# A multi-query attention kernel whose instruction order is written down as tables, with five short stretches ordered anew

## The chip, the cores and the metric

One NeuronCore of one Trainium2 chip runs the whole program. The metric is the device time of one execution in microseconds. The kernel before has a median of 664.33 us over three runs (664.21 to 664.44).

A core has engines that each take their own instruction list in order: TensorE (PE, matrix products into eight PSUM banks), ScalarE (ACT), VectorE (DVE), GpSimd (POOL) and SyncE (SP, which here only starts transfers). They meet through semaphores. Transfers are carried out by 16 DMA engines.

## The reference

```python
def reference(A_x, A_wq, A_wk, A_wv, A_wo, B_x, B_w1, B_b1, B_w2, B_b2):
    def _A_ref(x, wq, wk, wv, wo):               # S=2048, D=640, H=32, Dh=20
        q = (x @ wq).reshape(B, S, H, Dh).transpose(0, 2, 1, 3)
        k = x @ wk                               # one key head for all 32 heads
        v = x @ wv
        scores = jnp.einsum("bhqd,bkd->bhqk", q, k) * (Dh ** -0.5)
        p = _softmax(scores, axis=-1)
        o = jnp.einsum("bhqk,bkd->bhqd", p, v)
        return o.transpose(0, 2, 1, 3).reshape(B, S, H * Dh) @ wo
    def _B_ref(x, w1, b1, w2, b2):               # F=1536
        h = jnp.einsum("bsd,df->bsf", x, w1) + b1
        r = jnp.where(h > 0, h, 0)
        return jnp.einsum("bsf,fd->bsd", r * r, w2) + b2
    xn = _layernorm(A_x)
    return A_x + _A_ref(xn, A_wq, A_wk, A_wv, A_wo) + _B_ref(xn, B_w1, B_b1, B_w2, B_b2)
```

Attention and a feed-forward layer work on the same normalised input, and both are added to it. Softmax over 32 x 2048 x 2048 scores is the bulk.

## The kernel before

**Tiles and units.** The queries are cut into four chunks of 512, the heads into eight groups of four. That makes 32 blocks, each with 16 key tiles of 128 keys. A block and a key tile make a *unit*, numbered 16 x block + key tile (0 to 511). A unit has four score tiles, one per head, of 128 keys x 512 queries, numbered 4 x unit + head. A score tile fills one PSUM bank.

**Two ways to the exponential.** Most tiles go to ScalarE: a pair of score matmuls fills two banks, and one instruction (line 1328) takes the exponential of both into two slots of the buffer `PT`. Four matmuls, one per head, then multiply a unit of `PT` with the values (`PT,vx` in the profile) into the accumulator of the block. The other 164 units, here called *sets*, go to VectorE: it evicts each of the four banks (line 1551) with a multiply, an add and a conversion to 16-bit integers, whose bits read as bf16 are a piecewise linear exponential. To smooth it, three *passes* add one, two and three quarters of an octave to those bits in further buffers: on POOL (`int64_add`, line 1571), two passes joined in one instruction (line 2121), or on VectorE (line 1572). Thus a set has four *terms*, 0 to 3, and the sum of the four, with weights 1, 1, 0.707 and 0.707 held in `vx` and `vxs`, is the exponential.

**Pair sums.** Each term costs TensorE a group of four matmuls. To save groups, term 0 may be added into term 1, and term 3 into term 2, before they are multiplied. This is done by an accumulating DMA that POOL issues (line 1588 for 0 into 1, line 2047 for 3 into 2, 512 KB each; line 2119 for both in one transfer of 1024 KB), or by an addition on VectorE.

**Names.** In what follows an instruction is named as the change's tables name it:
- `q:` a pair of score tiles for ScalarE, `d:unit.head` a score tile for VectorE, `a:` an exponential on ScalarE, `e:unit.head` an eviction on VectorE;
- `p:unit.j` a pass, `j:unit.2` the joined passes 2 and 3;
- `s:unit.0` and `s:unit.3` the sums of 0 into 1 and of 3 into 2, `b:unit.3` both in one transfer;
- `v:unit` the multiplication of a ScalarE unit with the values, `u:unit.term` that of one term. The reader of `s:108.0` is `u:108.1`, that of `s:366.3` is `u:366.2`;
- `fill` and `warm`: matmuls with zeros whose result does not matter. `FFN`, `FP`, `OUT`, `QC` and the like are the parts of the projections and of the feed-forward layer, which stand between the attention work.

All matmuls go through the helper in line 729, so all have that line in the profile.

**What sets the order.** While the program is built, a planner goes step by step through a modelled time: class `Op` (line 251) holds each instruction with its engine, duration and dependences, and tables of rules and priorities decide which instruction comes next on which engine. Its result is then rearranged by `PLAN`, one text of indices for each engine, which `unpack` (line 290, called at line 2086) turns into an order; further texts choose which variant of a sum or pass is used, and on which VectorE instruction a POOL instruction has to wait because the two share a port (`held`). Then `replay` (line 300, called at line 2146) goes through the order with modelled durations and landings of transfers, and gives out PSUM banks, `PT` slots and term buffers. From the dependences the program derives the waits.

Landings there are a model, with constants near the head of the file:

```python
ADLATE = 0.6
ADLEAD = 1.24
ADLAND = 4.36
ADGAP = 2.73
```

Of the kernel before, what the change touches and what calls it, by code (L numbers as in the profile page):

```python
# [17 lines left out]
HPG = 4  # L18
# [20 lines left out]
def _pl(z):  # L39
# [9 lines left out]
NB = 7  # L49
PVB = 7  # L50
SHARED = (4, 5, 6)
SIDES = ((0, 1), (2, 3))
POOLED = tuple(range(NB))
HELD = sum(SIDES, ())
EVP = 0.8
JIT = 0.7
MRG = 9
M1 = 9
M1T = 0
ADDN = 0.5  # L60
R3 = 2
NOPEN = 2
SETW = HPG * 512
NL = 5
NT = 10
DRATE = 0.95
DLAST = 3.5
DSLACK = 0
URG = 4
PBIAS = 5  # L70
DGAP = 1.5
DMARG = 3.8
DMEND = 2.5
SLX = 5.0
CMX = 2.0
XRLAT = 6.2
NADS = 8
ADDUR = 0.905
ADPL = 0.3
ADM = 0.7  # L80
ADMP = 0.7
ADLATE = 0.6
ADLEAD = 1.24
SPF, SPG, SPT = 1.3, 0.84, 560.0
DWQ, DWO, DWB, DWS, DWM, DWOD, DOFF = 0.02, 0.22, 0.16, 0.02, 0.16, 1.0, 1.28
ADLAND = 4.36
ADGAP = 2.73
SWITCH = 0.0985
ACB, ACM = 0.0631, 0.4267
Q1POS = 3  # L90
WARM = 0.72

# [2165 lines left out]
```

## Time and profile before

| | |
|---|---|
| median of three runs | 664.33 us |
| profiled execution, first to last instruction | 663.4 us |
| TensorE busy | 655.2 us (99%) |
| ScalarE busy | 649.3 us (98%) |
| VectorE busy | 627.1 us (95%) |
| POOL busy | 533.1 us (80%) |
| single pair sums (512 KB), median from issue to landing | 5.7 us |
| double pair sums (1024 KB), median from issue to landing | 9.0 us |

The time of the runs lies 0.93 us above the span of the profiled execution; the rest lies before the first and behind the last instruction. In the rows, a line starts with a time or a source line, then the engine, the operation and the program's names `output<-input`; `xN` counts instructions, and what stands in brackets or behind the last bar is idle time of the engine just before them with what ended it. In rows of the timeline the first number is the start and the second the length of all the instructions of the row together.

### The profile page before, as it was taken

The numbers are of one execution on the slowest core, as the hardware profiler recorded it, in microseconds if no ns is written. First come the engines' busy times: TensorE is split into PE (matmuls) and PEld (weight loads), VectorE is DVE, ScalarE is ACT, GpSimd is POOL, SyncE is SP. The second block draws the span as 40 slices with busy tenths as digits, with TensorE's granted clock in tenths as the row PEclk, the third lists the DMA queues.
The fourth block names the chain that finished last, engine by engine and source line by source line (L and its number), as shares of the span: only waits on it lengthen the run. The fifth ranks groups of instructions, "written<-read, shape, count | busy, mean of one in ns | idle before, by whom it ended". The sixth has DMA issues, their size and how long they took to land. (4 is left out here: it accounts for less than half of the span.)

```text
span 663.4 us, 22377 instructions
## 1 busy us (share of the span) xinstructions
PE 655.2 (99%) x9569; PEld 211.9 (32%) x9570; DVE 627.1 (95%) x1125; ACT 649.3 (98%) x719; POOL 533.1 (80%) x528
## 2 busy tenths in 40 slices
PE   8999999999999999999999999999999999999997
PEld 4432222332322223323332222333333322223444
DVE  8979999999999999999999999999999999999997
ACT  7999999999999999999999999999999999999995
POOL 1629899898998889898999988889899999799300
PEclk9999999999999999999999999999999999999999
DMA  8594957788997995696957645798788655858741
GB/s 289 160 241 109 197 119 161 163 183 189 190 191 162 185 179 117 127 182 125 181 105 154 126 91 102 154 180 176 151 170 167 131 126 97 172 104 182 136 111 70
DMA packets 53528, 102.09 MB, mean 154 GB/s; under 512 B 15916, under 2 KB 31164, under 8 KB 53364
## 3 DMA queue, kind: packets, MB, share of 16 engines
q0 software_dynamic: 18544, 68.17, 55.5%
q1 hardware_dynamic: 34164, 31.94, 16.6%
q8 instruction: 75, 1.23, 0.8%
q10 hardware_dynamic: 720, 0.54, 0.3%
q14 instruction: 25, 0.20, 0.1%
HBM read 23.26 MB, written 10.01 MB: 50 GB/s over the span
## 5 line engine op out<-in xcount | busy, mean ns | idle before, releaser
L1328 ACT ACTIVATE PT<-ps 128x1024 bf16<-128x1024 f32 x696 | 640.3, 1121 | 2.2 <-PE ps L729 1.7
L1551 DVE TENSOR_SCALAR tx<-ps 128x512 uint16<-128x512 f32 x656 | 424.0, 683 | 21.1 <-PE ps L729 14.2
L1571 POOL INT64_ADD tx<-tx x369 | 391.2, 1130 | 57.3 <-PE ps L729 16.8
L729 PE MATMUL ps<-qT,kT 20*128 20x512 bf16 x2048 | 262.9, 384 | 0.3
L729 PEld LDWEIGHTS ps<-qT,kT 20*128 20x128 bf16 x2048 | 67.3, 91 | 253.3 <-ACT PT L1328 132.9
L729 PE MATMUL ps<-PT,vx 128*32 128x512 bf16 x1392 | 131.3, 384 | 0.0
L729 PE MATMUL ps<-tx,vxs 128*32 128x512 bf16 x1220 | 112.9, 384 | 0.4 <-DMA tx<-tx 0.3
L1588 POOL DMA_DIRECT2D tx<-tx x103 | 102.8, 998 | 7.7 <-POOL tx L1571 6.9
L729 PE MATMUL ps<-w_sb,big 128*32 128x320 bf16 x1536 | 82.6, 302 | 0.0
L729 PE MATMUL ps<-tx,vx 128*32 128x512 bf16 x864 | 81.0, 384 | 1.6 <-DMA tx<-tx 1.6
L729 PE MATMUL ps<-xnT,w_sb 128*32 128x512 bf16 x960 | 78.9, 383 | 0.0
L1572 DVE TENSOR_SCALAR tx<-tx 128x2048 uint16<-128x2048 uint16 x91 | 63.3, 707 | 0.8 <-DMA tx<-tx 0.5
L729 PEld LDWEIGHTS ps<-PT,vx 128*32 128x32 bf16 x1392 | 34.3, 94 | 39.7 <-issue 35.2
L729 PEld LDWEIGHTS ps<-w_sb,big 128*32 128x32 bf16 x1536 | 34.0, 95 | 31.1 <-issue 20.3
L729 PEld LDWEIGHTS ps<-tx,vxs 128*32 128x32 bf16 x1220 | 28.5, 94 | 36.5 <-issue 27.6
L1054 DVE TENSOR_SCALAR hT_tmp<-ps,b1col 128x512 bf16<-128x512 f32 x48 | 35.7, 743 | 1.6 <-PE ps L729 1.3
L729 PE MATMUL ps<-xnT,wq_sb 128*32 128x512 bf16 (+2 forms) x480 | 35.6, 356 | 0.0
L729 PE MATMUL ps<-wo_c,OC 128*32 128x320 bf16 x576 | 31.8, 301 | 0.0
L2121 POOL INT64_ADD tx<-tx x16 | 30.6, 1913 | 0.5
L729 PEld LDWEIGHTS ps<-tx,vx 128*32 128x32 bf16 x864 | 20.9, 95 | 27.9 <-issue 20.5
L729 PEld LDWEIGHTS ps<-xnT,w_sb 128*32 128x32 bf16 x960 | 19.3, 94 | 25.7 <-issue 17.4
L1416 DVE COPY OR<-ps 128x512 f32<-128x512 f32 x30 | 20.5, 682 | 0.9 <-PE ps L729 0.6
(91 smaller groups left out, 242.6 us busy)
## 6 DMA issues: line engine op xcount, KB each, us to landing
tx<-tx POOLq DMA_DIRECT2D x111, 512.0 KB, 5.7
tx<-tx POOLq DMA_DIRECT2D x7, 1024.0 KB, 9.0
w_sb<-in_B_w_dram SPq DMA_DIRECT2D x8, 480.0 KB, 9.4
big<-OR SPq DMA_DIRECT2D x71, 40.0 KB
xb<-in_A_x_dram SPq DMA_DIRECT2D x1, 2560.0 KB, 12.2
xb<-b2r POOLq DMA_DIRECT2D x1, 2560.0 KB, 19.0
xr<-xb SPq DMA_DIRECT2D x16, 160.0 KB, 3.4
out_dram<-out_sb SPq DMA_DIRECT2D x15, 160.0 KB, 2.9
```

The source lines that it names most:

```text
L729: return lambda e: e.matmul(out_(), l, val(r), start=val(start), stop=val(stop), tile_position=tp, skip_group_check=loose)
L1054: o = Op(f"RL{qc}_{f}", "DVE", 0.66, [lambda e: e.tensor_scalar(out=hT_tmp[:, k % 2, :], in0=ps[:, at(bk), :], scalar1=b1col[:, f:f + 1], ...
L1328: o = Op(f"ACT{st_['j']}", "ACT", ACB + ACM * n, [lambda e: e.activation(out=PT[:, slots[0].n:slots[0].n + n, :], in_=src(), func=AF.Exp, ...
L1416: tn = op(f"TN{b}", "DVE", 0.60, lambda e: e.tensor_copy(out=OR[:, a, :], in_=ps[:, PVB, :]), [lastpv] + or_users[a], prio=0)
L1551: d1 = op(f"D1_{n}_{i}", "DVE", 0.60, lambda e: e.tensor_scalar(out=L()[:, cs].bitcast(U16), in0=ps[:, ref.n, :], scalar1=XA, scalar2=XB, ...
L1571: fns = dict(POOL=lambda e, T=T, j=j: e.int64_add(out=T().bitcast(I64), in0=L().bitcast(I64), in1=TSTEP * j * 0x0001000100010001), DVE=lam ...
L1572: DVE=lambda e, T=T, j=j: e.tensor_scalar(out=T().bitcast(U16), in0=L().bitcast(U16), scalar1=TSTEP * j, scalar2=None, op0=ALU.add))
L1588: p = op(f"AD{a}_{n}", "POOL", ADDUR, lambda e, src=src, dst=dst: e.dma_start(dst(), src(), accum_op=ALU.add), dp + [ad_last.get(k)], dma= ...
L2121: fn = lambda e, x=x: e.int64_add(out=two(*sorted((x["ref"][2].n, x["ref"][3].n))).bitcast(I64), in0=two(*sorted((x["ref"][0].n, x["ref"][ ...
```

## The change

The planner, its rules and `PLAN` are removed, and so is `replay`. In their place stand tables of words: `ORDER` has, for each engine, every instruction by name in its order, with the PSUM banks, `PT` slots or term buffers behind an `@`; `TENANTS` lists for each of the 15 term buffers which terms live in it one after the other; `HELD` has, for each POOL instruction that shares the port, the VectorE instruction that it waits for. Dependences are rebuilt from these. To leave out waits that other waits already cover, the program still needs one order over all engines; it takes it from rough durations.

Nearly everywhere the words stand in the order of before. In five stretches, about 143-172, 227-250, 277-298, 449-470 and 470-491 us of the profile before, TensorE, VectorE, POOL and SP have another order, found by a search in which landings of the sums as recorded took the place of the modelled ones. In detail:
- POOL, in the first four stretches (before, then after):

```
p:108.1 p:110.3 s:108.0 p:109.2 p:107.1 p:108.2 p:106.1 p:109.3 s:107.0 p:106.2 p:107.2 s:106.0 p:106.3 p:127.1 p:126.1 s:127.0
p:108.1 j:108.2 s:108.0 p:110.3 p:109.2 p:109.3 p:106.2 p:107.1 p:106.1 s:107.0 s:106.0 p:106.3 s:127.0 p:107.3 p:126.1 p:126.3 s:126.0

j:172.2 b:172.3 p:171.1
j:172.2 s:172.0 s:172.3 p:171.1

p:222.1 b:222.3 p:223.3 p:221.3 p:220.1
p:222.1 p:223.3 s:222.3 p:221.3 p:221.1 s:222.0 p:221.2 p:220.1 j:220.2 p:219.1 s:220.0

p:367.1 p:367.3 s:367.0 p:365.3 s:366.0 p:365.2 p:366.3 p:364.2 s:365.0 p:364.3 s:366.3 p:364.1
p:367.1 p:366.3 s:367.0 p:367.2 p:366.1 s:366.0 j:365.2 p:364.1 p:366.2 s:365.0 s:366.3 j:364.2
```

- The number of double sums falls from seven to five, that of single sums by DMA rises from 111 to 116. A sum `s:382.3` is new.
- TensorE: score tiles, products and projections are interleaved anew in the stretches, with some other banks; `u:382.3` falls away. Three fills, at 39.33, 40.65 and 597.18 us, are left out.
- VectorE: nine times two evictions become one instruction over two banks, 128 x 1024 (`e:107.32`, `127.01`, `126.23`, `125.32`, `124.10`, `219.01`, `239.31`, `399.02`, `398.30`). Some passes move between VectorE and POOL.
- ScalarE: near 483 us, three pairs in a row (`a:1490`, `a:1492`, `a:1494`) are divided anew over the same six tiles, as three, two and one (`a:1491`, `a:1493`, `a:1495`).

The diff, cut to its core:

```diff
-RC = dict(SAME=0.0027, CR=0.105, RC=0.0995, FIRST=0.011, LANE=0.004, ACT=0.9035, ACTN=0.0165, ...
-def replay(seq, pool, order_all, upool):
...
+ORDER = {
...
+        "p:172.1@14 s:173.0 j:172.2@9,12 s:172.0 s:172.3 p:171.1@11 p:171.2@5 p:171.3@13 p:173.2@4 p:173.3@5 s:171.0 p:191.1@8 s:190.0 p:190.2@0 s:191.0 p:191.2@4 p:189.1@12 p:189.3@5 "
...
+        "p:366.3@0 s:367.0 p:367.2@7 p:366.1@14 s:366.0 j:365.2@6,2 p:364.1@12 p:366.2@7 s:365.0 s:366.3 j:364.2@6,10 p:363.1@2 j:363.2@12,5 p:383.3@1 p:383.1@6 s:363.0 s:383.0 p:382.1@7 "
...
+TENANTS = (
...
+HELD = (
...
-            if e in PLAN:
...
-                seq[e] = [old[k] for k in unpack(PLAN[e], len(old))]
...
+        for _, a, e, ns in planned("e"):
+            u, hs = int(a.split(".")[0]), [int(h) for h in a.split(".")[1]]
+            x = sets.setdefault(u, Terms())
+            i, n = len(x.order), len(hs)
+            refs = [head[HPG * u + h][0] for h in hs]
...
+        for k, a, e, _ in planned("s", "b"):
+            u, j = map(int, a.split("."))
+            x = sets[u]
+            pairs = ((0, 1), (3, 2)) if k == "b" else ((0, 1),) if j == 0 else ((3, 2),)
+            deps = [d for p in pairs for t in p for d in x.made[t]] + (x.reads[1] if j == 0 else [])
...
+        seq = {e: [made[w] for w in names[e]] for e in ENG}
...
+        filler = {(u, j): o for e in ("DVE", "POOL") for o in seq[e] for u, j in o.fills}
+        for n, tenants in enumerate(TENANTS):
+            free_after = list(xn_op.values()) if n >= NMORE else []
+            for k in map(int, tenants.split()):
+                u, j = divmod(k, NTERM)
+                assert sets[u].at[j] == n
+                filler.pop((u, j)).deps += free_after
+                free_after = sets[u].reads[j]
...
+        ROUGH = dict(PE=0.22, ACT=0.95, DVE=0.6, POOL=1.0, SP=0.6)
...
+            free[o.eng] = t + ROUGH[o.eng]
+            when[o] = free[o.eng] + (0.2 if o.dma is None else 4.0)
+            order_all.append(o)
```

More of the change, by code (lines that the diff above doesn't have):

```diff
@@ L48 @@
 PTR = 16
-NB = 7
-PVB = 7
+NSET = 15
+SETW = HPG * 512
 SHARED = (4, 5, 6)
[L52 to L76, printed above, removed]
-NADS = 8
[L78 to L84, printed above, removed]
@@ new lines, in bass_parallel_sum__grouped_kv_mqa__dense_activation_squared_relu__prompt_kernel, with col4, evac_T @@
+        lib_op = op("LIB", "POOL", lambda e: e.load_library(library_config.all_libraries[1]), list(xn_op.values()))
+        def col4(lhs, rhs, n, k, last, bank, m=32, loose=False):
+            return [mm(lambda j=j: ps[32 * j:32 * j + m, at(bank), 0:n], lhs(j), rhs, k == 0, last, (0, 32 * j), loose) for j in range(4)]
+        def evac_T(st, bk, eng, t):
+            cs = slice(128 * st, 128 * st + 128)
+            src = lambda: psbf(bk)[:, 0:DT * 128].rearrange("p (dt n) -> p dt n", dt=DT)
+            if eng == "DVE":
+                te_op[st] = op(f"TE{st}", "DVE", lambda e: e.tensor_copy(out=xnT[:, :, cs], in_=src()), [t])
+            else:
+                te_op[st] = op(f"TE{st}", "ACT", lambda e: e.activation(out=xnT[:, :, cs], in_=src(), func=AF.Identity), [t])
+            return te_op[st]
@@ new lines, in scaled_v, with unit @@
+        def scaled_v(c):
+            cs = slice(4 * c, 4 * c + 4)
+            vs_of[c] = op(f"VS{c}", "DVE", lambda e: e.tensor_scalar(out=vxs[:, cs, :], in0=vx[:, cs, :], scalar1=TW[2], scalar2=None, op0=ALU.mult), [v_of[c]], lock=True)
+        scaled_v(0)
+        def unit(name, chunks, deps, ref):
+            for k, fn in enumerate(chunks):
+                o = op(f"{name}.{k}", "PE", fn, deps if k == 0 else [])
+                if k == 0:
+                    o.takes = [ref]
+            return o
@@ L1926, in bass_parallel_sum__grouped_kv_mqa__dense_activation_squared_relu__prompt_kernel @@
-        assert not misc and unit[0] is None and act_next[0] == len(steps), (len(misc), misc[:1] and misc[0].name, act_next[0], len(steps), pv_blk, cur)
-        assert pv_blk[0] == NBLK and not dve_q and not pool_q and not sp_q, (dve_q, pool_q, sp_q)
-        assert len(fin_ev) == 8
-        MODEL.update(end=max(free.values()), lastact=act_ops[-1].fin, sets=len(sets), steps=len(steps), busy={k: sum(o.dur for o in seq[k]) for k in ENG}, seq=seq, order=order_all)
-        if STOP:
-            raise StopIteration
@@ new lines, in bass_parallel_sum__grouped_kv_mqa__dense_activation_squared_relu__prompt_kernel @@
+        for o in made.values():
+            o.deps = [x for d in o.deps for x in (same[id(d.dma), d.tgt[1]] if d.dma is not None else [d])]
+        giver = {}
+        for o in made.values():
+            for r in o.gives:
+                giver[r] = o
+        bank_rel = dict(first_rel)
+        for o in seq["PE"]:
+            assert len(o.takes) == len(o.banks)
+            for r, n in zip(o.takes, o.banks):
+                r.n = n
+                if n in bank_rel:
+                    o.deps.append(bank_rel[n])
+                bank_rel[n] = giver[r]
```

1943 lines of the change are left out of this document (402 added, 1541 removed), and 445 rows, old and new, of tables (HELD, ORDER, PLAN, TENANTS).

## The prediction

> **What bounds the kernel now.** I read the page first: the busy time of each engine, the granted clock, the groups, the sums.
>
> ```profile
> span 663.4 us, 22377 instructions
> PE 655.2 (99%) x9569; PEld 211.9 (32%) x9570; DVE 627.1 (95%) x1125; ACT 649.3 (98%) x719; POOL 533.1 (80%) x528
> PEclk9999999999999999999999999999999999999999
> ...
> L1328 ACT ACTIVATE PT<-ps 128x1024 bf16<-128x1024 f32 x696 | 640.3, 1121 | 2.2 <-PE ps L729 1.7
> L1551 DVE TENSOR_SCALAR tx<-ps 128x512 uint16<-128x512 f32 x656 | 424.0, 683 | 21.1 <-PE ps L729 14.2
> ...
> tx<-tx POOLq DMA_DIRECT2D x111, 512.0 KB, 5.7
> tx<-tx POOLq DMA_DIRECT2D x7, 1024.0 KB, 9.0
> ```
>
> TensorE and ScalarE are both full: between 20 and 650 us they are busy 627.41 and 628.01 of 630 us.
>
> ```profile
> core 0: us, PE busy (x) PEld busy (x) DVE busy (x) ACT busy (x) POOL busy (x), PEclk, DMA share, GB/s
> ...
> 20.00:650.00 630.00, 627.41 (x9014) 196.14 (x9003) 599.79 (x1038) 628.01 (x684) 529.38 (x518) 1.00 0.74 151
> ```
>
> TensorE writes scores, ScalarE takes the exponential of most of them and hands the bank back, TensorE multiplies the result: neither can run away from the other. What either loses in the middle is therefore lost at the end. Next the list of waits: which transfers did TensorE wait for?
>
> ```profile
> PE ps L729 <- DMA tx<-tx: 1.9, 4, 0.6
> ...
> PEld ps L729 <- DMA tx<-tx: 3.5, 5, 1.0
> ```
>
> Four times, 1.9 us in all, it waited for a pair sum (an accumulating transfer from `tx` to `tx`); its weight load also waited a fifth time. The timeline of TensorE finds them; the readers are `u:106.1`, `u:172.1`, `u:222.2` and `u:366.1`. The fifth, `u:108.1` at 156.2 us, cost TensorE almost nothing.
>
> ```profile
> 164.29 0.40 PE L729 MATMUL ps<-tx,vx 128*32 128x512 bf16 x4 [0.64 <-DMA tx<-tx]
> ...
> 239.71 0.40 PE L729 MATMUL ps<-tx,vx 128*32 128x512 bf16 x4 [0.31 <-DMA tx<-tx]
> ...
> 292.17 0.40 PE L729 MATMUL ps<-tx,vxs 128*32 128x512 bf16 x4 [0.31 <-DMA tx<-tx]
> ...
> 463.80 0.40 PE L729 MATMUL ps<-tx,vx 128*32 128x512 bf16 x4 [0.62 <-DMA tx<-tx]
> ```
>
> The chain of waits goes through the last of these: 8.34 us from issue to landing, and from there on TensorE alone.
>
> ```profile
> 455.42 8.34 DMA tx<-tx
> 463.76 0.04 issue
> 463.80 49.98 PE ps L729 x737
> ```
>
> **The change part by part.** *The bookkeeping* (planner, rules and index tables out, word tables in) runs while the program is built and issues no instruction: 0. Outside five stretches, about 143-172, 227-250, 277-298, 449-470 and 470-491 us of the profile, the four engines and SP's queue have their words in the same order as before, so what follows concerns these, and three fills.
>
> *The five waits.* What do they cost both engines? ScalarE's rows around the two long ones:
>
> ```profile
> 162.49 1.96 ACT L1328 ACTIVATE PT<-ps 128x1024 bf16<-128x1024 f32 x2
> 165.09 1.94 ACT L1328 ACTIVATE PT<-ps 128x1024 bf16<-128x1024 f32 x2 [0.64 <-PE ps L729]
> ...
> 462.09 2.02 ACT L1328 ACTIVATE PT<-ps 128x1024 bf16<-128x1024 f32 x2
> 464.60 1.02 ACT L1328 ACTIVATE PT<-ps 128x1024 bf16<-128x1024 f32 x1 [0.48 <-PE ps L729]
> ...
> 469.20 26.73 ACT L1328 ACTIVATE PT<-ps 128x1024 bf16<-128x1024 f32 x29
> ```
>
> An unbroken run of 29 takes 26.73 us; the last lasts 1.12, so one step is (26.73 - 1.12) / 28 = 0.915 us. Two steps took 165.09 - 162.49 = 2.60 and 464.60 - 462.09 = 2.51 us, which is 0.77 and 0.68 over 1.83. With 0.31 each for the short ones, as TensorE shows them, the cost is 2.07 us. Bounds: 1.9 (TensorE's own wait) and 3.5 (its weight load's, which would partly have idled anyhow). I take 2.0.
>
> Does each of the five go? The new order either issues the sum earlier, puts the reader later, or makes it smaller.
> - `s:366.0`: issued at 455.42 as before, or up to 1 us later; its reader `u:366.1` goes about 4.8 us down TensorE's list, so to about 463.8 - 0.8 + 4.8 = 467.8 us. With the slowest single sum here, 9.7 us (below), it lands at 466.1. Gone.
> - `b:222.3`, both sums of the unit in one 1024 KB transfer, becomes `s:222.3`, with `s:222.0` several instructions later. 512 KB at 5.7 us from 284.4 (two passes behind the old 282.35) lands at 290.1; the reader `u:222.2` comes near 290.9. Gone, with 0.8 us to spare.
> - `b:172.3` becomes `s:172.0` and, right behind, `s:172.3`, but the reader of the first moves up by three ScalarE steps, to 239.71 - 0.5 - 2.86 = 236.4 us.
>
> ```profile
> 229.52 1.22 POOL L2119 DMA_DIRECT2D tx<-tx  x1 [0.30 <-POOL tx L2121]
> ...
> DMA to landing us min/median/max: 4.5/5.7/9.7
> ...
> DMA to landing us min/median/max: 8.5/9.0/10.1
> ```
>
>   These are the single sums of L1588 and the double ones of L2119. From 229.52 a single one lands at 235.2, or up to 1.6 later where the second shares its bytes: 236.8. New wait 0 to 0.5.
> - `s:106.0` moves from 156.75 to right behind `s:107.0`, near 155.3, with that one near 154.4 (six passes of 1.04 after `s:108.0`, where there were five before 153.10). Two sums of 512 KB in a row are the bytes of one double: 154.4 + 9.0 = 163.4 (162.9 to 164.5). The reader stands near 164.1. New wait 0 to 0.5.
> - `s:108.0` stays; the reader gets about 0.6 us.
>
> *The new tight place.* `s:366.3` now stands directly behind `s:365.0`, and its reader `u:366.2` moves up.
>
> ```profile
> 460.67 1.03 POOL L1588 DMA_DIRECT2D tx<-tx  x1
> 461.73 1.05 POOL L1571 INT64_ADD tx<-tx  x1
> 462.71 0.91 POOL L2047 DMA_DIRECT2D tx<-tx  x1
> ...
> 471.15 0.39 PE L729 MATMUL ps<-tx,vxs 128*32 128x512 bf16 x4
> ```
>
> Before, the issues were 2.04 us apart and the reader followed at 471.15. Now it comes 1.3 us earlier in the list and 0.8 by the removed wait: 469.0. The pair is issued from about 460.4 (one joined pass takes the place of two single ones) and lands as a double does at 469.4 (468.9 to 470.5). New wait 0 to 1.5, middle 0.4. Behind it in TensorE's queue stand score groups, so ScalarE loses the same time.
>
> The new waits may thus cost 0 to 2.5 us; I take 0.3, as two of three middles lie ahead of their readers.
>
> [...]
>
> *TensorE's work.* Three fills leave, at 39.33, 40.65 and 597.18 us, four matmuls each.
>
> ```profile
> 39.33 0.40 PE L729 MATMUL ps<-kT,zeros 128*32 128x512 bf16 x4
> 39.56 0.39 PE L729 MATMUL ps<-xnT,wq_sb 128*32 128x512 bf16 x4
> ...
> 597.18 0.39 PE L729 MATMUL ps<-kT,zeros 128*32 128x512 bf16 x4
> ...
> 599.05 41.68 ACT L1328 ACTIVATE PT<-ps 128x1024 bf16<-128x1024 f32 x45
> ```
>
> From start to start a fill is 39.56 - 39.33 = 0.23 us, 0.69 for three. ScalarE hides the last: behind it, 45 steps at (41.68 - 1.12) / 44 = 0.92 us are its own pace. The first two lie in the opening, where it waits elsewhere too. 0 to 0.69; I take 0.1. In the last two stretches a new sum `s:382.3` saves one group, and two score groups merge with others: 0.44 us less. There ScalarE is at the 0.915 of its unbroken run, which hides it: 0 to 0.44, taken 0.1. Elsewhere the groups are the same in number. ScalarE's work is the same: near 483 us six tiles in three instructions, before as after: 0.
>
> *VectorE.* Nine pairs of evictions become one instruction of 128x1024.
>
> ```profile
> 454.18 1.96 DVE L1551 TENSOR_SCALAR tx<-ps 128x512 uint16<-128x512 f32 x3
> ...
> L1139 DVE TENSOR_TENSOR out_sb<-ps,xr 128x320 bf16<-128x320 f32 x24 | 11.6, 484 | 1.6 <-PE ps L729 1.1
> ```
>
> No row has that shape. From (683 - 484) / 192 = 1.04 ns per element, 1024 elements give about 1.21 us. Two in a row take 0.64 + 0.683 = 1.32. Each saves 0.1 us on an engine that is busy 95% and off the chain there; but the first bank is free up to 1.21 - 0.68 = 0.5 us later. Bounds for nine: -1.0 and +4.8 us; taken 0, because the list puts other score groups between.
>
> *SP and POOL* issue the same transfers, seven doubles becoming five with five more singles, and some of SP's a few us later. No row shows TensorE waiting for one of SP's there: 0.
>
> The sum: -2.0 + 0.3 - 0.1 - 0.1 = -1.9 us against 663.4 profiled. The median of the runs, 664.33, lies 0.9 above the span; the same shift gives 662.4.
>
> **The rivals.**
>
> *Waits moved, not removed.* `s:366.3` lands late by 0.8 or more, `s:172.0` and `s:106.0` by 0.2 each. For it: three sums are left within 0.7 us of their readers, and landings scatter over 5 us. Against: the middle values clear two. -2.0 + 1.2 - 0.1 = -0.9: 663.4.
>
> *Nothing measurable.* The landings of the profile do not repeat, and five others would be late in another execution; or ScalarE, at 98%, would soon have stopped TensorE anyway. Against: everything after each wait is shifted rigidly, as neither engine has idle time to take it up, and the three runs lie within 0.23 us. 664.3.
>
> *Slower, by the joint evictions.* Both banks of a joint instruction come free at its end, 0.5 us later than the first did. If the next score group for ScalarE waits for that bank, TensorE and ScalarE both stop. It decides from 1.9 / 9 = 0.21 us each. The row for evictions shows that VectorE already waits for TensorE (14.2 us), so banks are not in surplus. Against: 683 ns of VectorE per bank hardly ever shows as TensorE's own wait. At 0.35 each: +3.2 - 1.9 = +1.3, so 665.6.
>
> **How the numbers follow.** Forecast 662.4: 0.58. Waits moved, 663.4: 0.22. Nothing, 664.3: 0.10. Slower, 665.6: 0.10. The forecast's own range: its low end has 2.07 us gone, no new wait, and all of the fills and merged groups but the fill that ScalarE hides (0.69 + 0.44 - 0.23 = 0.90): 661.4; its high end has new waits of 0.9 instead of 0.3: 663.0. The whole range takes in the second and third: 661.4 to 664.4. About 0.2% (1.3 us) is what can be told from no change, so faster means below 663.0: nearly all of the forecast (0.56) and a fifth of the second (0.04) make 0.60; the rest of these and the third 0.30; slower 0.10.
>
> **What would show it.** Right: the list of waits has TensorE waiting for `tx<-tx` under 0.8 us in total, none at the four readers; ScalarE's two long gaps are gone; whatever lies behind 491 us is 1.5 to 2.3 us earlier. Waits moved: a new row with a wait for a transfer near 469, 236 or 164 us. Slower: TensorE waiting for VectorE's evictions inside the stretches. My forecast is wrong if the late sums are gone and the end still does not move, or if some engine that I costed at nothing shows a new gap over 0.5 us.

## The result, and the profile after

| | before | after |
|---|---|---|
| median of four executions | 664.38 us (664.21 to 665.63) | 672.18 us (671.35 to 672.76) |
| profiled execution, first to last instruction | 663.4 us | 670.4 us |
| TensorE's waits for pair sums | 1.9 us, 4 times | none |
| mean granted clock of TensorE in the four executions after | | 0.989 to 0.995 |

The change makes the kernel slower: ratio 1.011 (1.0093 to 1.0127), 7.8 us, where 1.9 us less had been forecast. An execution over 1.5% slower than the fastest of its kernel is left out of the medians and ratios in this document.

The page after, with the lines that answer to those of before:

```profile
span 670.4 us, 22264 instructions
PE 659.8 (98%) x9553; PEld 213.4 (32%) x9554; DVE 624.1 (93%) x1111; ACT 650.1 (97%) x719; POOL 538.8 (80%) x531
PEclk9999999999999999999999999999879999999999
...
L1071 ACT ACTIVATE PT<-ps 128x1024 bf16<-128x1024 f32 x696 | 641.0, 1126 | 7.8 <-PE ps L599 7.1
L1081 DVE TENSOR_SCALAR tx<-ps 128x512 uint16<-128x512 f32 (+1 forms) x647 | 423.0, 690 | 27.3 <-PE ps L599 19.9
...
tx<-tx POOLq DMA_DIRECT2D x116, 512.0 KB, 5.8
tx<-tx POOLq DMA_DIRECT2D x5, 1024.0 KB, 9.0
```

ScalarE works as long as before (641.0 for 640.3 us), but now stands for TensorE 7.1 us where it stood 1.7. TensorE's granted clock has a dent in two of 40 slices (8 and 7 tenths), at 470 to 500 us; before it was full throughout. TensorE's waits:

```profile
PE ps L599 <- DVE tx L1081: 2.5, 2, 1.4
...
PE ps L599 <- DMA qT<-QCr: 0.8, 1, 0.8
```

No wait for `tx<-tx` is left in this execution: all five late sums are gone. In their place are two waits for VectorE's evictions and one for a transfer of queries. The timeline of TensorE has them at three places:

```profile
170.07 0.39 PE L599 MATMUL ps<-qT,kT 20*128 20x512 bf16 x3 [1.01 <-DVE tx L1081]
...
480.19 0.39 PE L599 MATMUL ps<-qT,kT 20*128 20x512 bf16 x3 [1.44 <-DVE tx L1081]
...
482.86 0.61 PE L599 MATMUL ps<-qT,kT 20*128 20x512 bf16 x3 [0.75 <-DMA qT<-QCr]
```

From the third on, three matmuls take 0.61 us and no longer 0.39: the clock is halved, 0.50 for 1.00. The windows around it (the columns as in the prediction; the clock is the third number from the end):

```profile
482.50:483.00 0.50, 0.14 (x3) 0.14 (x3) 0.50 (x2) 0.09 (x1) 0.50 (x2) 0.59 0.96 186
483.00:492.50 9.50, 9.50 (x79) 1.98 (x76) 4.37 (x6) 6.33 (x6) 6.90 (x8) 0.50 0.73 151
492.50:493.00 0.50, 0.50 (x10) 0.05 (x2) 0.45 (x1) 0.25 (x1) 0.20 (x2) 0.67 0.13 14
```

That is 0.41 + 9.5 + 0.33 = 10.2 us at half clock, in which TensorE is busy nearly all the time and ScalarE only two thirds of it. What ScalarE loses is in its own rows:

```profile
480.65 1.94 ACT L1071 ACTIVATE PT<-ps 128x1024 bf16<-128x1024 f32 x2 [1.70 <-PE ps L599]
483.51 1.02 ACT L1071 ACTIVATE PT<-ps 128x1024 bf16<-128x1024 f32 x1 [0.92 <-PE ps L599]
484.97 1.02 ACT L1071 ACTIVATE PT<-ps 128x1024 bf16<-128x1024 f32 x1 [0.44 <-PE ps L599]
486.32 1.02 ACT L1071 ACTIVATE PT<-ps 128x1024 bf16<-128x1024 f32 x1 [0.33 <-PE ps L599]
488.30 2.11 ACT L1071 ACTIVATE PT<-ps 128x1024 bf16<-128x1024 f32 x2 [0.95 <-PE ps L599]
491.30 1.45 ACT L1071 ACTIVATE PT<-ps 128x1536 bf16<-128x1536 f32 x1 [0.89 <-PE ps L599]
493.38 8.85 ACT L1071 ACTIVATE PT<-ps 128x1024 bf16<-128x1024 f32 x10 [0.63 <-PE ps L599]
```

The first two gaps belong to the two waits, 2.62 us; the other five, 3.24 us, to the half clock. With some 0.13 us more for each interrupted step (the prediction's 0.77 for a gap of 0.64) the seven cost 6.8 us. The shift of equal instructions between the traces agrees: by ScalarE's instructions 0.5 us earlier than before at 478 us, 6.2 us later behind 493 and at the end (TensorE's last matmuls start at 665.97 for 659.75). The other 0.8 of the 7.0 us by which the span grows lie behind the last matmuls.

**Why the eviction is late.** VectorE's timeline and POOL's:

```profile
479.44 0.69 DVE L1081 TENSOR_SCALAR tx<-ps 128x512 uint16<-128x512 f32 x1 [1.74 <-DMA tx<-tx]
```

```profile
469.44 1.76 POOL L1118 DMA_DIRECT2D tx<-tx  x2
...
475.21 2.26 POOL L1118 DMA_DIRECT2D tx<-tx  x2
...
477.64 1.76 POOL L1118 DMA_DIRECT2D tx<-tx  x1
```

`e:378.0` writes into the term buffer from which `s:383.0` still reads. That sum is the second of two issued back to back from 469.4 on and lands 9.3 us after its issue. TensorE, which needs the bank behind the eviction, stands. Three more, `s:382.3`, `s:382.0` and `s:381.0`, go out between 475.2 and 478 and land after 8.5, 10.5 and 11.2 us. The median of the five singles issued in 468 to 480 us is 9.3 us, where all 116 have 5.8:

```profile
tx<-tx POOLq DMA_DIRECT2D x5, 512.0 KB, 9.3
```

**Why the queries are late.** The chain of waits after goes through SP, and SP's timeline shows where it stood:

```profile
462.45 0.33 SPq L943 DMA_DIRECT2D drs<-R  x1
468.82 1.39 SPq L964 DMA_DIRECT2D big<-drs  x2
...
473.60 3.80 SPq L799 DMA_DIRECT2D qT<-QCr  x3
```

```profile
462.45 6.36 DMA drs<-R
...
473.60 1.46 SPq L799
...
475.10 7.62 DMA qT<-QCr
...
482.86 27.26 PE ps L599 x344
```

The transfer of queries `QD24_1`, which `d:399.2` reads, stands in the new order behind one that has to wait for `RS20` (`drs<-R`, 6.36 us). Before, SP issued it at 457.68, ahead of that:

```profile
457.68 1.26 SPq L1034 DMA_DIRECT2D qT<-QCr  x1
462.35 0.33 SPq L1423 DMA_DIRECT2D drs<-R  x1
466.68 1.42 SPq L1445 DMA_DIRECT2D big<-drs  x2
```

**Why the first wait.** In the first stretch `OM4_3+` went down SP's list, from 157.1 to 160.4 us. An instruction of VectorE, `CM0_2`, waits for it, and with it every eviction behind it:

```profile
168.72 0.69 DVE L971 TENSOR_TENSOR OC<-cmore 128x512 bf16<-128x512 f32 x1 [1.23 <-DMA big<-OR]
```

### The profile page after: what moved, and what is told of

Same layout as the page of the kernel before. It is cut to its first block, busy times and chain, and to the rows that moved or that the text cites. A ratio compares the mean times of both kernels' runs of the same rounds, so it can differ in the third digit from the quotient of the medians.

```text
span 670.4 us, 22264 instructions
## 1 busy us (share of the span) xinstructions
PE 659.8 (98%) x9553; PEld 213.4 (32%) x9554; DVE 624.1 (93%) x1111; ACT 650.1 (97%) x719; POOL 538.8 (80%) x531
## 4 chain that ended last, share of the span: by engine, by line
PE 89%; DMA 4%; ACT 2%; DVE 2%; SPq 2%; issue 1%
PE ps L599 88%; ACT PT L1071 2%; DMA drs<-R 2%; DMA big<-OR 1%; DMA qT<-QCr 1%; SPq L964 1%; SPq L799 1%; PE ps L699 0%; PE ps L1029 0%; PE ps L702 0%; DVE tx L1081 0%; DVE big L676 0%; SPq L958 0%; DVE OR L661 0%; SPq L941 0%
## 5 line engine op out<-in xcount | busy, mean ns | idle before, releaser
L1071 ACT ACTIVATE PT<-ps 128x1024 bf16<-128x1024 f32 x696 | 641.0, 1126 | 7.8 <-PE ps L599 7.1
L1081 DVE TENSOR_SCALAR tx<-ps 128x512 uint16<-128x512 f32 (+1 forms) x647 | 423.0, 690 | 27.3 <-PE ps L599 19.9
L1094 POOL INT64_ADD tx<-tx x364 | 390.3, 1152 | 55.6 <-DVE big L835 13.6
L599 PE MATMUL ps<-qT,kT 20*128 20x512 bf16 x2048 | 266.2, 386 | 3.9 <-DVE tx L1081 2.5
L599 PE MATMUL ps<-PT,vx 128*32 128x512 bf16 x1392 | 132.7, 386 | 0.0
L1118 POOL DMA_DIRECT2D tx<-tx x121 | 122.8, 1034 | 11.0 <-POOL tx L1094 6.2
L599 PE MATMUL ps<-w_sb,big 128*32 128x320 bf16 x1536 | 80.9, 302 | 0.0
L1095 DVE TENSOR_SCALAR tx<-tx 128x2048 uint16<-128x2048 uint16 x86 | 60.6, 717 | 0.2
L1100 POOL INT64_ADD tx<-tx x21 | 40.7, 1937 | 1.0 <-PE ps L599 0.3
```

The source lines that it names most:

```text
L599: return lambda e: e.matmul(out_(), l, val(r), start=val(start), stop=val(stop), tile_position=tp, skip_group_check=loose)
L1071: o = op(f"a:{a}", e, lambda e, qk=qk, slots=slots: e.activation(out=some(PT, slots), in_=some(ps, [r.n for r in qk.takes]), func=AF.Exp, ...
L1081: o = op(f"e:{a}", e, lambda e, x=x, i=i, n=n, refs=refs: e.tensor_scalar(out=x.ref(0)[:, i * 512:(i + n) * 512].bitcast(U16) if n == 1 el ...
L1094: fn = dict(POOL=lambda e, x=x, j=j: e.int64_add(out=x.ref(j).bitcast(I64), in0=x.ref(0).bitcast(I64), in1=TSTEP * j * 0x0001000100010001) ...
L1095: DVE=lambda e, x=x, j=j: e.tensor_scalar(out=x.ref(j).bitcast(U16), in0=x.ref(0).bitcast(U16), scalar1=TSTEP * j, scalar2=None, op0=ALU.a ...
L1100: o = op(f"j:{w}", e, lambda e, x=x: e.int64_add(out=two(*sorted((x.at[2], x.at[3]))).bitcast(I64), in0=two(*sorted((x.at[0], x.at[1]))).b ...
```

## The experiments

After reading the traces the theory was: the waits in the last stretch (for the sum, for the queries) cost what they show, and set off a fall of the clock that costs more. The first rival was that the joint evictions or the denser stretch cost it and the waits are by the way; the second, that the loss is spread over all five stretches.

### Taking the waits away one by one

`e1_q` puts the queries right behind `RS20` in SP's list; `e2_sum` puts `s:363.0` ahead of a pass in POOL's, so that `s:383.0` no longer follows it back to back; `e3_both` does both.

```diff
 e1_q, SP
-RS20 BC20_3 BC20_0 QD24_2 BC19_1 SL21 QD25_2 QD24_1 QD26_0
+RS20 QD24_1 BC20_3 BC20_0 QD24_2 BC19_1 SL21 QD25_2 QD26_0
 e2_sum, POOL
-j:363.2 p:383.3 p:383.1 s:363.0 s:383.0
+j:363.2 s:363.0 p:383.3 p:383.1 s:383.0
```

> The changed kernel with one transfer of SP's queue moved: the slice of queries QD24_1 goes from behind QD25_2 to right behind RS20, so it is issued near 462.8 us instead of 475.1. My theory: TensorE's wait for it (0.75 us at 482.9) goes, TensorE's wait of 1.44 us at 480.2 stays, and whether the clock falls decides the time. If 1.44 us of idle TensorE alone bring the clock down, about 671.3 us; if it takes both waits, the clock stays at 1.0 and the time is about 664.4 - 0.65 (what the changed kernel is ahead at 478 us) + 1.6 = 665.3. Rival (the joint evictions or the mix of work in the last stretch bring the clock down, not the waits): about 671.4, with the clock low between 482 and 493 us.

> The changed kernel with one sum of POOL's queue moved: s:363.0 stands right behind j:363.2, two passes ahead of s:383.0, instead of directly before it. My theory: s:383.0 then lands near 470.3 + 5.7 = 476 us instead of 479.3, the eviction e:378.0, which needs its buffer, no longer waits 1.74 us, and TensorE's wait at 480.2 goes. But TensorE now comes to d:399.2 near 480.5 and finds the queries QD24_1 landing only near 482.7: a wait of about 2.2 us in one piece, so the clock falls all the same: about 671 to 672 us. Rival (only the first wait brings the clock down): 664.4 - 0.65 + 2.2 = 666. Rival (joint evictions): 671 with the clock low and no long wait.

> Both moves. My theory: no wait of TensorE for these two in the last stretch, clock 1.0 throughout, and the changed kernel keeps what it is ahead at 478 us: 664.4 - 0.65 = 663.7, or down to 663.2 with the fewer groups of the last stretch; the first stretch's wait of 1.0 us (for CM0_2 behind OM4_3+) stays. Rival (the joint evictions or the mix bring the clock down or hold banks): over 668 us.

Measured: `e1_q` 671.57 us (1.0122, 1.0093 to 1.0151), `e2_sum` 673.56 (1.0148, 1.0113 to 1.0182), `e3_both` 669.57 (1.0068, 1.0047 to 1.009). Each did away with its own wait, but alone neither gave a time below 671 us. The first came out as its theory has it for a wait of 1.44 us alone; its rival gives the same time. The second has a long wait, as forecast, but not the one forecast, and the third misses its 663.7 by 6 us. In `e2_sum` (first row) and `e3_both` (second) a pass of POOL is late in place of the eviction:

```profile
487.13 0.62 PE L599 MATMUL ps<-tx,vxs 128*32 128x512 bf16 x4 [2.15 <-POOL tx L1094]
```

```profile
486.20 0.40 PE L598 MATMUL ps<-tx,vxs 128*32 128x512 bf16 x4 [1.60 <-POOL tx L1093]
```

In `e3_both` POOL stood before it for a sum that had not landed, `s:382.0`, whose source buffer `p:379.3` wants to write; `p:378.3`, for which TensorE waits, is behind that:

```profile
484.10 4.07 POOL L1093 INT64_ADD tx<-tx  x4 [1.91 <-DMA tx<-tx]
```

So it is the same fault one place further: not a late sum's reader, but the next tenant of its source buffer. Each of the three profiles has a fall of the clock at a wait; that of `e1_q` has two, one of them in the first stretch, where TensorE waited 1.66 us at 170.7 us (1.01 in the kernel after, which kept its clock there). The single executions separate the two costs: those of `e3_both` at a mean clock of 1.0 took 667.1 and 667.5 us, at 0.990 672.3; of `e1_q` 671.3 and 671.6 at 0.995, and 676.2 at 0.985.

### The clock apart from the waits

`e5_keep` is the kernel after with matmuls by zeros, added to open accumulators, in the two places where TensorE stood; `v:362` and two `OUT12` pieces change places with it. The waits stay, and something runs in them.

```diff
-OUT12 OUT12 v:362 OUT12 OUT12 d:378.3@7 d:378.2@5
+OUT12 OUT12 OUT12 OUT12 d:378.3@7 keep:22 keep:22 keep:22 keep:22 keep:22 v:362 d:378.2@5
...
-u:383.3@7 u:383.1 d:399.2@5
+u:383.3@7 u:383.1 keep:23 keep:23 keep:23 d:399.2@5
```

> The changed kernel with both waits left in, but TensorE given something to do in them: five groups of matmuls with zeros ahead of d:378.2 (v:362 and two pieces of OUT12 change places with them) and three ahead of d:399.2, added into accumulators that are open, so the result is the same. It tells what the waits cost by themselves from what the lower clock costs. My theory (the clock falls because TensorE is idle): clock 1.0, and the time is that of the waits alone, 664.4 - 0.65 + 1.44 + 0.75 and some tenths = 666 us. Rival (the clock falls for the mix of work, or for too much work): 671 or more.

Measured: 669.99 us (668.01 to 674.11; 1.0097, 1.0069 to 1.0125). The two places of the profiled execution, which took 668.01:

```profile
478.27 1.26 PE L599 MATMUL ps<-kT,zeros 128*32 128x512 bf16 x20
...
480.18 0.39 PE L599 MATMUL ps<-qT,kT 20*128 20x512 bf16 x3 [0.43 <-DVE tx L1084]
...
481.92 0.82 PE L599 MATMUL ps<-kT,zeros 128*32 128x512 bf16 x12
```

```profile
478.00:500.00 22.00, 20.29 (x308) 6.97 (x308) 16.24 (x25) 18.35 (x20) 16.93 (x18) 1.00 0.84 168
```

The clock stays full, and the execution is 4.2 us shorter than the median after. A further wait of 1.28 us at 488 us is left uncovered, and two of the four executions lost clock all the same (0.995: 671.29; 0.990: 674.11). The forecast of 666 us was thus missed, by 4 us in the median and by 2 at full clock. The two executions at full clock, 668.01 and 668.69, put the half clock at about 4 us of the 7.8; the rest is the waits and the first stretch.

### Going on to the end of the row

`e6_three` is `e3_both` with `p:378.3` and `p:380.2` ahead of `p:379.3` on POOL. `e7_four` also puts `OM4_3+` ahead of `BC4_3` on SP, for the first stretch. `e8_split` is that with the nine joint evictions divided again.

```diff
 e6_three, POOL
-s:379.0 p:379.3@4 p:378.3@6 p:380.2@3 p:379.2@9
+s:379.0 p:378.3@6 p:380.2@3 p:379.3@4 p:379.2@9
 e7_four, SP
-XR2 BC4_3 OM5_0 QD9_0 BC4_0 OM4_3+ SL5
+XR2 OM4_3+ BC4_3 OM5_0 QD9_0 BC4_0 SL5
 e8_split, VectorE (one of nine)
-e:399.02@14
+e:399.0@14 e:399.2
```

> Both moves, and a third: in POOL's queue the passes p:378.3 and p:380.2 go ahead of p:379.3, which in the run with both moves stood at 482.2 to 484.1 us waiting for the sum s:382.0 to leave its buffer; behind it p:378.3 was late and TensorE waited 1.6 us for it at 486.2, after which the clock was 0.5 for 7 us. My theory: with that wait gone the clock is 1.0 in the last stretch and the kernel keeps the 0.65 us that it is ahead at 478 us: 664.8 - 0.65 = 664.2, down to 663.5; the first stretch's wait of 1.0 us stays, and in executions where it brings the clock down the time is about 4 us more. Rival (each removed wait only uncovers the next one): 667 or more, with a further wait over 1 us in the last stretch.

> The three moves and a fourth, in the first stretch: in SP's queue OM4_3+ goes from behind BC4_0 to ahead of BC4_3, where SP stood still from 154.3 to 155.8 us waiting for RS4. My theory: OM4_3+ lands near 162 us instead of 168.7, CM0_2 on VectorE no longer waits 1.2 us, TensorE's wait of 1.0 us at 170.1 goes, and the time is about 1.1 us below that of the three moves, 663.0 (662.4 to 663.5): all five late sums gone, no new wait, which is what I had forecast for the change (2 us under before). Rival: the place where it stood idle isn't free (its readers hold it), no gain; 664.2.

> The four moves with the nine joint evictions taken apart again, two of 128x512 each, in the same places. My rival of the prediction had the joint ones cost 0.35 us each through the bank that comes free late; by it this kernel is 2 to 3 us faster than the four moves alone. My theory now: they cost or save less than 0.5 us in all, so the same time within 0.5 us; or, where VectorE has no time to spare, up to 1 us slower (0.1 us each).

Measured: 667.09 (1.0037, 1.0024 to 1.005), 667.57 (1.0045, 1.0033 to 1.0057) and 668.68 us (1.0076, 1.0052 to 1.0101). `e6_three` takes away about 5 of the 7.8 us with three moved words, and its rival had it right: a further wait was uncovered. `e8_split` has the span of `e7_four` in the profile, 665.4 us, and its median is 1.1 us longer, with five of six executions below full clock: the joint evictions cost nothing that shows, and this half of the first rival falls. In `e7_four` the wait at 170 us shrinks from 1.01 to 0.33, yet nothing is gained, and its 663.0 is missed by 4.6 us: the trace gives it back by 188 us, where a pass on VectorE takes 1.5 us instead of 0.8. Two passes of POOL run beside it there, from 177.60 to 180.27 us; before, they had ended at 179.00. And the fault has moved on once more, to `e:398.30`, which waits for `s:381.0`:

```profile
487.86 1.22 DVE L1080 TENSOR_SCALAR tx<-ps 128x1024 uint16<-128x1024 f32 x1 [2.32 <-DMA tx<-tx]
```

```profile
489.14 0.60 PE L598 MATMUL ps<-qT,kT 20*128 20x512 bf16 x5 [1.61 <-DVE tx L1080]
```

`e9_sum` therefore takes the root: `e6_three` without the new sum `s:382.3`, whose term TensorE multiplies by itself again, so that two sums stand where three did.

```diff
 POOL
-p:382.2@3 p:383.2@10 s:382.3 s:382.0
+p:382.2@3 p:383.2@10 s:382.0
 TensorE
-u:383.3@7 u:383.1 d:399.2@5
+u:383.3@7 u:383.1 u:382.3 d:399.2@5
```

> The changed kernel with the last two stretches mended: the two moves in SP's and POOL's queues and the passes p:378.3 and p:380.2 ahead of p:379.3, as before, and the new sum s:382.3 taken out again (u:382.3 is multiplied on TensorE behind u:383.1). Without it two sums of 512 KB stand between 475 and 479 us instead of three. My theory: s:381.0 then lands near 485 us instead of 488, before the eviction e:398.30 needs its buffer at 486, no wait over 1 us is left in the last stretch, the clock stays at 1.0 there, and the time comes down to that of the first three stretches alone, 665.75, or some tenths less. Rival (a further wait shows up): 666.5 or more.

Measured: 666.27 us (1.0027, 1.0015 to 1.0038), 0.5 us above the forecast and 0.2 below its rival. The stretch of 478 to 500 us is clean, without a gap of TensorE and at full clock:

```profile
478.00:500.00 22.00, 22.00 (x332) 7.75 (x329) 19.14 (x30) 21.63 (x25) 19.59 (x20) 1.00 0.78 154
```

The profiled execution itself took 668.68 us: it lost clock elsewhere, at 14.4 us, behind a wait of 1.71 us in the opening (0.61 in the kernel after). The median is within 0.6 us of the kernel with the last two stretches as before (`m1_first3b`, below). So what they lost came from sums in a row whose source buffers are wanted again within 10 us, from the order of the passes behind them, and from the queries. The mix of work is nearly the same in this kernel and the clock stays full there, so the other half of the first rival falls too.

### The stretches by themselves, and the order of before in the new form

First four kernels, which could not tell: `m1_first3` (new order in the first three stretches), `m2_last2` (in the last two), `m3_23` (in the second and third) and `clk` (the order of before with one late pass, see below). Their table `HELD` leaves out 60, 94, 105 and 154 of POOL's 403 to 405 waits for VectorE, and names earlier instructions in 34 to 122 others.

> The tables of the change, but with the order of before in the last two stretches (the tables are joined at 409 us, where both orders agree; buffers are renumbered to fit). My theory: the loss of the change is in the last two stretches alone. In the changed kernel's trace TensorE stands 0.18 us ahead of before at 441 us, so this one comes out at 664.7 - 0.2 = 664.5 (664.2 to 665.0), though three late sums are gone: the first stretch gives back what it gains by its wait for CM0_2. In executions in which that wait grows past about 1.4 us the clock falls and 2 to 4 us are lost. Rival (the tables themselves, without planner and replay, cost time through other waits): 666 or more.

> The other half: the order of before up to 409 us, the new one in the last two stretches. My theory: from the changed kernel's trace the loss between 441 and 490 us is 6.25 + 0.17 = 6.4 us, so 664.7 + 6.4 = 671.1 (668 to 673, as the clock's share varies from execution to execution). Rival (the loss needs what the first stretches do to the landings): below 667.

> The new order in the second and third stretches only, that of before in the first, fourth and fifth. My theory: the changed kernel's trace gains 0.43 and 0.28 us in these two, each about the wait of TensorE that my prediction had taken away there (0.31 each) and little more, and no wait takes its place, so 664.7 - 0.7 = 664.0 (663.6 to 664.4). Rival (gains of that size are given back by landings that differ from execution to execution): 664.7.

> The order of before throughout, written as tables, with one wait added at a quiet place: a piece of the feed-forward layer on TensorE (FFN1_11.1, at 420.5 us) also waits for the pass p:333.1 on POOL, which ends near 422.4. It measures what one wait of TensorE of about 2 us costs by itself, with nothing else changed. My theory (an idle TensorE brings the clock down to 0.5 for some microseconds): 664.7 + 2 for the wait + 1.5 to 5 for the clock = 668 to 672, and a granted clock of 0.5 behind the wait. Rival (the clock fell for the mix of work in the last stretch): 664.7 + 2 = 666.7 and clock 1.0.

Measured: 702.2, 706.94, 716.1 and, from a single execution, 726.4 us. The times follow the waits left out, not the stretches. What such a wait spares can be read in `m1_first3`, in a pass of VectorE that runs beside two of POOL's:

```profile
454.38 0.69 DVE L1096 TENSOR_SCALAR tx<-tx 128x2048 uint16<-128x2048 uint16 x1
...
456.86 2.88 DVE L1096 TENSOR_SCALAR tx<-tx 128x2048 uint16<-128x2048 uint16 x1
```

```profile
456.55 2.63 POOL L1095 INT64_ADD tx<-tx  x2
```

The same pass takes 0.69 us where POOL's next one starts 0.11 us before its end (at 454.96), and 2.88 us beside two. This is what the runs show of the port that VectorE and POOL share by the section on the kernel before; no row names a port. The same questions with the whole table, and the order of before in table form (`m0_old`):

> The first three stretches in the new order, the last two in the old one, again, now with the waits that keep POOL's passes and VectorE's passes apart (the table HELD) taken from before completely; the run that left 40 of them out showed a VectorE pass of 2.9 us instead of 0.7 next to POOL's, and 700 us. My theory is the same as for that run: the changed kernel stands 0.18 us ahead of before at 441 us, so 664.7 - 0.2 = 664.5 (664.2 to 665.0), and 2 to 4 us more in executions in which the first stretch's wait brings the clock down. Rival (the tables without planner and replay cost time by themselves): 666 or more.

> The new order in the second and third stretches only, again, with all the waits between POOL and VectorE. My theory: 664.7 - 0.43 - 0.28 = 664.0 (663.6 to 664.4), since neither stretch showed a new wait in the changed kernel's trace. Rival: landings that differ from execution to execution give it back, 664.7.

> The order of before throughout, written as tables; nothing else. It tells what the tables by themselves cost, and is the base for the runs that mix the two orders. My theory: the same as before, 664.5 (664.2 to 665.0). Rival (the tables cost a few tenths, which would explain why three moved readers gave no gain): 665.0 to 665.5.

| | stretches with the new order | time, us | ratio |
|---|---|---|---|
| `m0_old` | none | 665.09 | 1.0005 (0.9995 to 1.0015) |
| `m3_23b` | 2, 3 | 664.65 | 1.0005 (0.9996 to 1.0014) |
| `m1_first3b` | 1, 2, 3 | 665.75 | 1.0014 (1.0004 to 1.0024) |
| after | all | 672.18 | 1.011 (1.0093 to 1.0127) |

The forecasts of 664.5 for `m1_first3b` and 664.0 for `m3_23b` are both missed upwards; the second came to its rival's 664.7. The form of tables costs nothing that shows, and the second and third stretch change nothing that shows. With the first it is 1.2 us slower than before (664.54 beside it), and the last two cost 672.18 - 665.75 = 6.4 us. This is a difference: no run with the whole table has the last two alone. But for the 1.2 us of the first stretch, the second rival falls.

`m5_readers` earns the waits in the cheapest way: the order of before, with only the readers `u:172.1`, `u:222.2`, `u:222.1` and `u:366.1` further down TensorE's list. `m7_best` joins the move of `u:366.1` with the new second and third stretch.

```diff
 m5_readers, TensorE (one of three)
-v:354 u:366.1 d:383.3@6 q:1424,1425@0,1 OUT11 OUT11 OUT11 OUT11 q:1426,1427@3,4 d:382.0@5 OUT11 v:352
+v:354 OUT11 OUT11 d:383.3@6 q:1424,1425@0,1 OUT11 OUT11 v:352 q:1426,1427@3,4 d:382.0@5 u:366.1 OUT11
```

> The order of before throughout, as tables, with three readers moved and nothing else: u:172.1 goes 1.5 us further down TensorE's list, u:222.2 with u:222.1 0.7 us, u:366.1 1.5 us; other groups of the same lists take their places. All instructions, transfers and sums stay as before. It takes three of the five waits away without touching POOL, SP or VectorE. My theory: what a removed wait gives reaches the end if nothing else is moved, so 664.7 - 0.48 - 0.38 - 0.80 = 663.1 (662.8 to 663.7). Rival (ScalarE or a term buffer soon takes the time back): 664.3 or more.

> What gained in any of the runs: the second and third stretches in the new order, the rest in the old one, and u:366.1 moved 1.5 us down TensorE's list. My theory: the second and third stretches gain 0.4 to 0.7 in the traces and u:366.1 between 0 and 0.8, as its sum lands late only in some executions: 663.9 (663.3 to 664.6). Rival (what is gained there is lost at the end of the program, as in the run with three readers moved): 664.6.

Measured: 664.71 us (1.0006, 0.9997 to 1.0015) and 664.57 us (0.9997, 0.9988 to 1.0006). The waits are gone there too, but for that of `s:106.0`, which both leave (1.0 and 0.7 us). Neither is measurably faster, as the rivals had it. In the trace of `m5_readers` the 0.3 us gained at 293 us is given back by 298. In `m7_best` the median span is 0.7 us shorter than that of before on the same chip (662.4 to 663.1), but the time outside the span is 2.17 us instead of 1.84.

### One late pass, alone

`clk_b` is the order of before with one thing added: the matmul piece `FFN1_11` on TensorE waits for a pass of POOL, `p:333.1`.

```diff
+        made["FFN1_11.1"].deps.append("p:333.1")
```

> The order of before throughout, as tables with all the waits between POOL and VectorE, and one wait added: FFN1_11.1 on TensorE at 420.5 us also waits for the pass p:333.1, which ends near 422.4. My theory (an idle TensorE brings the clock down): about 2 us of waiting in one piece and then a granted clock of 0.5 for 3 to 10 us, 664.7 + 2 + 1.5 to 5 = 668 to 672. Rival (the clock fell for the mix of work in the last stretch): 664.7 + 2 = 666.7 and clock 1.0.

Measured: 667.78 us (1.0056, 1.0041 to 1.0071).

```profile
422.25 0.62 PE L599 MATMUL ps<-xnT,w_sb 128*32 128x512 bf16 x8 [1.91 <-POOL tx L1094]
```

The profiled execution kept the full clock and took 666.58, 2.0 us above before, for 1.9 us of wait. The other three had a mean clock of 0.997 and took 667.61, 667.96 and 668.98; of 27 executions of before beside them, two had 0.997 or less. So the added wait brought the clock down in three of four, for 1.0 to 2.4 us more. That is the mechanism of the theory, at a time just below its range.

## Why the prediction was wrong

**The failed step** is "SP and POOL issue the same transfers … No row shows TensorE waiting for one of SP's there: 0". That no row of before shows a wait says that the old places were early enough, not the new ones. `QD24_1` went down SP's list behind a transfer that stands 6.4 us for `RS20`, and `OM4_3+` by 3.3 us; neither was followed to its reader. On POOL's side each sum was followed to TensorE's reader alone. Its source buffer has a next tenant, too, and `e:378.0`, `p:379.3` and `e:398.30` waited for it in turn. The prediction lets two sums in a row land like a double, after 9.0 us, and `s:383.0` did so (9.3); but it worked this out only where a late one had been, and the last stretch, with a pair back to back and three in 2.4 us, was not gone through at all.

**The missing term** is what an idle TensorE does to its clock. Waits of 1.44 + 0.75 us were followed by 10.2 us at half clock. By the runs the 7.8 us are: about 4 for the half clock (672.18 less the 668.0 and 668.7 of `e5_keep` at full clock), about 2.6 for the waits of the last stretch (from there to `m1_first3b`; the wait of 1.28 us in `e5_keep` is in it), and 1.2 for the first stretch. The division is rough: the four executions after, from 671.35 to 672.76 us, do not follow their mean clocks. In other profiles single waits of 1.28 us (`e6_three`), 1.55 and 1.66 (`e1_q`), 1.60 (`e3_both`), 1.71 (`e9_sum`) and 2.15 us (`e2_sum`) came with a fall.

**The five waits, -2.0: right in the trace, not earned in the time.** The five late sums are gone as worked out one by one. But `m5_readers` and `m7_best`, which remove three of them (1.2 us by the prediction's rows) and do nothing else that costs, gained 0.4 us at the most by their medians, and the interval of the better one ends at 0.8. Part of it is that the profiled execution of before was not a median one: its time is its span and some 1.8 us, as in nearly every execution measured, so by estimate about 665.2 against a median of 664.4. The prediction read the difference between span and median as what lies outside the span. In other profiles with the old order of the first stretch `s:106.0` is late each time (TensorE waits 0.51 to 0.95 us); `s:366.0` is late in `m0_old` (0.78) and not in `clk_b` and `m3_23b`. The rival "nothing measurable" was half right on this, with a weight of 0.10.

**The tight sums, +0.3: at the low end of their bounds.** None of `s:366.3`, `s:172.0` and `s:106.0` kept TensorE waiting.

**Fills and fewer groups, -0.2; tables, 0:** no run has the fills or the groups alone; `m0_old` shows no cost of the tables.

**Joint evictions, 0: right.** A 128x1024 one took 1.22 us (1.21 estimated), and dividing all nine left the span where it was.

**What would make it wrong** was named: the late sums gone and the end not moving, or a new gap over 0.5 us on an engine costed at nothing. Both came: the sums went and the end came later, and an eviction of VectorE and a transfer of SP, both costed at 0, kept TensorE waiting for 1.44 and 0.75 us. The rival that ended slower had the joint evictions for its cause, which cost nothing that shows.

**Open:** whether POOL's later passes are all that gives back the first stretch's gain in `e7_four`, and why `m3_23b` and `m7_best` have 0.3 to 0.4 us more outside their span.

## What to carry to other kernels

When an order is changed, follow each moved transfer to all that waits for it: its reader, the next writer of the buffer it reads from, and what stands behind a waiting issue in the same queue. Where TensorE is full, as here, a wait of 1.3 to 2.2 us can have a price beyond its length, since in some executions (1.28 us in `e6_three`, 2.15 in `e2_sum`) it came with a clock of 0.50 for 3.4 us or more; so an order that removed four waits of 0.3 to 0.6 us and added waits of 1.4 and 0.8 lost. One profiled execution is no list of late transfers: see in several which waits repeat, and set the span against the median before spending effort on them.

## What the runs showed of the hardware

In these profiles the half clock comes in steps of about 3.41 us. `e6_three` with the step ahead, then `e3_both` and `e1_q`, each at or behind its wait:

```profile
486.59:490.00 3.41, 2.13 (x32) 0.66 (x32) 2.56 (x4) 2.59 (x5) 3.11 (x4) 1.00 0.65 151
490.00:493.41 3.41, 3.41 (x34) 0.65 (x26) 3.24 (x5) 2.46 (x3) 2.07 (x3) 0.50 0.91 173
```

```profile
487.00:495.00 8.00, 8.00 (x70) 1.77 (x68) 4.47 (x7) 5.69 (x6) 4.90 (x6) 0.57 0.66 138
```

```profile
172.00:176.00 4.00, 4.00 (x39) 0.72 (x37) 2.94 (x6) 3.06 (x4) 3.25 (x5) 0.57 0.74 183
...
483.00:499.00 16.00, 16.00 (x128) 3.33 (x129) 8.06 (x11) 10.50 (x11) 8.83 (x9) 0.50 0.74 149
499.00:503.00 4.00, 4.00 (x59) 1.19 (x56) 3.77 (x6) 3.55 (x4) 2.50 (x3) 0.85 0.00 0
```

`e6_three` has 3.41 us at half clock. A mean of 0.57 over 8 us is 0.43 x 8 x 2 = 6.9 us at half; over 4 us it is 3.4; the last two rows make 17.2, and the kernel after had 10.2: one, two, one, five and three times 3.4 us. The mean clocks of whole executions have the same steps (1.0, 0.997, 0.995, 0.992, 0.990; the 0.999 of `e5_keep` is a fall behind the last matmuls). By a straight line through their executions a step costs 1.25 us in `e3_both` and 1.44 in `e5_keep`. How many steps follow is not settled: 1.55 us of wait (`e1_q`) was followed by five, 1.28 us (`e6_three`) by one, 1.61 (`e7_four`), 1.40 (`e8_split`) and another 1.28 us (`e5_keep`) by none. So the 1.4 us in the expectation of `m1_first3` is no limit that shows. TensorE was busy nearly all through the slow steps (16.00 of 16.00 us from 483 to 499 in `e1_q`, 9.97 of 10.24 in the kernel after).

The traces also show where the falls lie. In four profiles the falls of one execution lie whole numbers of 3.413 us apart (10.24 / 3, from the three steps of the kernel after): 91 in `e1_q`, where they begin at 172.50 and 483.12 us, 55 in the kernel after (482.59 and 670.33), 54 in `e2_sum` (486.36 and 670.68) and 53 in `e3_both` (487.34 and 668.24); in the last three the later one is behind the last matmuls. In the seven falls of the profiles after, `e1_q`, `e2_sum`, `e3_both`, `e6_three` and `e9_sum`, TensorE was busy 1.7 to 2.1 of 3.41 us in the step ahead (1.92 in the kernel after, 2.13 in `e6_three`). In `e7_four`, where the clock stayed full, no row shows where such a step would begin. One that began at 488.58 would divide the wait of 1.61 us, with 2.36 us busy ahead of it and 2.85 in it; this is not shown. Nor does a rule follow: the clock stayed full in `clk_b`, too, at 1.74 busy, and in `e8_split` with a wait of 1.40 us. `e7_four`, then `clk_b`:

```profile
485.17:488.58 3.41, 2.36 (x31) 0.60 (x23) 1.09 (x2) 3.28 (x4) 3.41 (x4) 1.00 1.05 211
```

```profile
418.60:422.01 3.41, 1.74 (x31) 0.58 (x23) 2.43 (x5) 2.92 (x4) 2.88 (x3) 1.00 0.62 128
```

Accumulating sums of 512 KB land after 4.5 us at the least (`s:` sums of line 1588 before), but after 8.5 to 11.2 where three are issued in 2.4 us (after); and a pass of VectorE took 2.88 instead of 0.69 us beside two of POOL's (`m1_first3`).
